# Gated layers in 50 units of 510 tokens across all batches, in place of 56 units of 448

## The chip, the core and the metric

The kernel runs on one core of one Trainium2 chip. The core has five engines with an instruction queue each: PE (matrix multiplication, called TensorE), ACT (ScalarE), DVE (VectorE), POOL (GpSimd) and SP (SyncE), which here issues nearly all DMAs. Sixteen DMA engines carry the transfers. The metric is the device time of one launch in microseconds (us); lower is better. Three runs of the kernel before took 1591.54, 1593.37 and 1595.23 us, median 1593.37.

## The reference

Eight batches of 3136 tokens with 256 columns pass through a filter in the frequency domain and then a gated layer; only the essence is shown.

```python
X = np.fft.rfft(x, axis=1)                      # x: (8, 3136, 256)
y = np.fft.irfft(X * (filt_r + 1j * filt_i), n=3136, axis=1)
h = np.maximum(y @ w_in, 0.0)                   # w_in: (256, 1024)
hp = pad(h, 1 token of zeros at both ends of each batch)
conv_out = sum(conv_w[k] * hp[:, k:k + 3136] for k in range(3))
out = (h / (1 + np.exp(-conv_out))) @ w_out     # w_out: (1024, 256)
```

## The kernel before

The Fourier transforms are done as matrix products in four passes over a batch, each pass in 14 pieces `q`. Pass "1" reads `x` and stores to `a_dram`; pass "2" reads that back, multiplies by the filter (`filt`, three DVE operations and one POOL addition); pass "3" stores to `b_dram`; pass "4" reads that and gives `y`, the input of the gated layer, kept on chip as a coarse and a fine half (`y` is two tiles, and so are the weights `wi`, `wo` and the gated values `g`, so that one product takes three matmuls, `mm3`). An operation of a pass is called by its number below: a 2 is one piece of the second pass.

The first batch is transformed alone (the head). After that the transforms of the following batches are interleaved with the gated layer. The gated layer is cut into units of `SUB` = 448 tokens, seven to a batch and 56 in all, and each unit into eight blocks `f` of 128 hidden columns. One (unit, `f`) is a **step** `m` of the main loop, 448 steps in all. In step `m`

- PE does the transform operations that the table `plan` puts on this step, then the six matmuls of `inner` (128x450, into a PSUM bank of `ps_h`, four of them), then `project` for step `m - 6`: three matmuls for each tile of 128 tokens, accumulated over the eight `f` in the two banks of `ps_o`.
- ACT does `relu` and `centre` for step `m - 1`, `sigmoid` for `m - 2`, `round_g` for `m - 3`; DVE does `tap`, `gate`, `tap`; POOL does `rest_g` for `m - 4`. The tile `t` that they share has four buffers, so `centre` waits until `rest_g` of four steps earlier is done.
- At the head of a step, `evacuate` copies the finished `ps_o` of a unit whose last `f` was projected in the step before (DVE, two copies) and SP stores it; then `from_bank` empties the transform banks that the step before filled (DVE for a 2 or a 4, ACT for a 1 or a 3, which SP then stores). There are two such banks, `ps_t`.

448 is 3.5 tiles of 128, so two units share a middle tile: its first 64 columns come from the even unit, the last 64 from the odd one (`split_parts`, tiles `gm`). Even units project three tiles, odd ones four. Within a batch of 56 steps, the 2s stand on every second step and the 3s on those between.

All engines follow the order in which the code is written (`manual_schedule`). SP issues loads ahead: the inputs of five operations ahead (`want_in`), the tables for 1 and 3 three such operations ahead (`want_table`), the filter for the next 2 (`want_filter`). A load that reads what a pass stored is issued only when all 14 stores of that pass have landed (`ready`). A DMA on SP also waits for the DMA eight places before it to land: they share a completion semaphore, DMAHW0 to DMAHW7 in turn.

Of the kernel before, what the change touches and what calls it, by code (L numbers as in the profile page):

```python
# [124 lines left out]
def tile_fft_filter_gated_ffn(  # L125
# [25 lines left out]
    def lo_pool(dst, src, hi):  # L151
        nc.gpsimd.tensor_tensor(out=dst, in0=src, in1=hi.bitcast(F32), op=ALU.subtract)  # L152
# [276 lines left out]
    outv = out.rearrange("b s d -> (b s) d").rearrange("(j t p) d -> j p t d", p=128, t=NT)  # L429
    hs, ts, gs, mids, pos = {}, {}, {}, {}, {}  # L430
    NU = B * NSUB
    HALF = SUB - 3 * 128

    def at(m):

        return (m // NF, m % NF) if 0 <= m < NF * NU else None

    def inner(u, f):
        ps = ps_h.tile([128, 512], F32, name="ps_h")[:, 0:SUB + 2]
        fs = slice(128 * f, 128 * f + 128)  # L440
        yh, yl = ys[u // NSUB]
        us = slice(u % NSUB * SUB, u % NSUB * SUB + SUB + 2)
# [5 lines left out]
        nc.scalar.activation(hs[u, f], hs[u, f], AF.Relu)  # L448

    def centre(u, f):  # L450
        ts[u, f] = t = wp.tile([128, SUB], F32, name="t", bufs=4)
        nc.scalar.activation(t, hs[u, f][:, 1:SUB + 1], AF.Copy, scale=cw[:, 1, f:f + 1])  # L452

    def tap(u, f, k):
        h, t = hs[u, f], ts[u, f]
        nc.vector.scalar_tensor_tensor(out=t, in0=h[:, k:SUB + k], scalar=cw[:, k, f:f + 1], in1=t, op0=ALU.mult, op1=ALU.add)  # L456

    def sigmoid(u, f):
        nc.scalar.activation(ts[u, f], ts[u, f], AF.Sigmoid)  # L459

    def gate(u, f):
        nc.vector.tensor_mul(ts[u, f], hs.pop((u, f))[:, 1:SUB + 1], ts[u, f])  # L462

    def split_parts(u, f):

        if u % 2:
            return ((gs[u, f], slice(0, 384), slice(HALF, SUB)), (mids[u // 2, f], slice(HALF, 128), slice(0, HALF)))
        return ((gs[u, f], slice(0, 384), slice(0, 384)), (mids[u // 2, f], slice(0, HALF), slice(384, SUB)))

    def round_g(u, f):  # L470
        gs[u, f] = [wp.tile([128, 384], F32R, name=f"g{h}", bufs=4) for h in range(2)]
        if u % 2 == 0:
            mids[u // 2, f] = [wp.tile([128, 128], F32R, name=f"gm{h}", bufs=NF) for h in range(2)]
        for g, o, i in split_parts(u, f):
            hi_act(g[0][:, o], ts[u, f][:, i])

    def rest_g(u, f):
        for g, o, i in split_parts(u, f):
            lo_pool(g[1][:, o], ts[u, f][:, i], g[0][:, o])
        del ts[u, f]  # L480

    def project(u, f):
        g = gs.pop((u, f))
        tiles = [[h[:, 128 * k:128 * k + 128] for h in g] for k in range(3)]
        if u % 2:
            tiles = [[h[:] for h in mids.pop((u // 2, f))]] + tiles
        if f == 0:
            pos[u] = [ps_o.tile([128, 512], F32, name=f"po{k}") for k in range(2)]
        for t, (gh, gl) in enumerate(tiles):
            o = pos[u][t // 2][:, t % 2 * D:t % 2 * D + D]  # L490
            first, last = f == 0 and t % 2 == 0, f == NF - 1
            nc.tensor.matmul(o, lhsT=gh, rhs=wo[0][:, f], start=first, stop=False, skip_group_check=True)  # L492
            nc.tensor.matmul(o, lhsT=gh, rhs=wo[1][:, f], start=False, stop=False, skip_group_check=True)  # L493
            nc.tensor.matmul(o, lhsT=gl, rhs=wo[0][:, f], start=False, stop=last, skip_group_check=True)  # L494

    def evacuate(u, f):
        if f < NF - 1:
            return
        t0, nt = (3, 4) if u % 2 else (0, 3)
        for k in range(2):  # L500
            n = min(2, nt - 2 * k)
            ot = wp.tile([128, 2, D], F32, name="ot", bufs=3)
            o, src = ot[:, 0:n].rearrange("p t d -> p (t d)"), pos[u][k][:, 0:n * D]
            if u == NU - 1 and k:
                nc.scalar.activation(o, src, AF.Copy)
            else:
                nc.vector.tensor_copy(o, src)  # L507
            nc.sync.dma_start(out=outv[u // 2][:, t0 + 2 * k:t0 + 2 * k + n], in_=ot[:, 0:n])

    NW = NF * NSUB  # L510
    plan = {}

    def put(m, kind, b, q):
        plan.setdefault(m, []).append((kind, b, q))

    for t in range(1, B):
        w = NW * (t - 1)
        at2, at4 = (10, [44 + 10 * q // NP for q in range(NP)]) if t == 1 else (4, [37 + 17 * q // NP for q in range(NP)])
        used = set(at4)
        for q in range(NP):  # L520
            used |= {at2 + 2 * q, at2 + 3 + 2 * q}
            put(w + at2 + 2 * q, "2", t, q)
            put(w + at2 + 3 + 2 * q, "3", t, q)
            put(w + at4[q], "4", t, q)
        if t == 1:
            for q in range(AHEAD, NP):
                s = (q - AHEAD) * 7 // (NP - AHEAD)
                used.add(s)
                put(s, "1", 1, q)
        free = [s for s in range(53) if s not in used]  # L530
        free = sorted(free + [s for s in range(at2, 53) if s // NF % 2 == 0 and s not in free][::-1][:NP - len(free)])
        if t + 1 < B:
            for q, s in enumerate(free[:NP]):
                put(w + s, "1", t + 1, q)
    order = [(m, op) for m in sorted(plan) for op in plan[m]]
    inputs = [op for _, op in order if op[0] in "124"]
    tables = [op for _, op in order if op[0] in "13"]
# [70 lines left out]
    with tc.manual_schedule(engines=COMPUTE | {mybir.EngineType.SP}):  # L608
# [4 lines left out]
        for m in range(NF * NU + PLAG + 1):  # L613
# [74 lines left out]
```

## Time and profile before

| what | value |
|---|---|
| median of three runs | 1593.37 us |
| profiled execution, device time | 1592.42 us |
| its span, first to last instruction | 1590.6 us |
| instructions | 28686 |
| granted TensorE clock, mean | 0.99 |
| first `inner` matmul | 120.5 us after the start of the span |

The span begins with the head, in which PE often waits, and goes on with 448 steps that are laid end to end on PE. [...] An operation on PE that stands in two parts in the records (transform matmuls of type f32) shows as twice as many rows.

```profile
PEclk9889999999999999999999999999999999999999
```

This row of the page, forty equal slices of the span, says that from the fourth slice on at least nine tenths of the clock were granted.

### The profile page before, as it was taken

How to read it: one execution, taken by the hardware profiler on the slowest of the kernel's cores; microseconds unless marked ns; L12 is line 12 of the kernel's file. 1: busy time of each engine (PE TensorE's matmuls, PEld its weight loads, DVE VectorE, ACT ScalarE, POOL GpSimd, SP SyncE). 2: the span in 40 equal slices, each digit the busy share in tenths (PEclk: the TensorE clock that was granted, in tenths of full speed). 3: DMA queues.
4: the chain of work that ended last, by engine and by line, in shares of the span. 5: the costliest groups of instructions: out<-in, count | busy, mean ns of one | idle time of the engine just before them, and what ended most of it. 6: DMA issues, size and time to landing. Idle time of an engine off the chain costs nothing.

```text
span 1590.6 us, 28686 instructions
## 1 busy us (share of the span) xinstructions
PE 1539.5 (97%) x9648; PEld 1395.2 (88%) x9648; DVE 1195.3 (75%) x1966; ACT 1197.6 (75%) x2623; POOL 877.1 (55%) x1170
## 2 busy tenths in 40 slices
PE   6879999999999999999999999999999999999999
PEld 5778889988899888998899988998889988899998
DVE  5856887578776887768776778667877788877876
ACT  3368668876788667986688766887668966799897
POOL 2523545745565454755556454664556655576554
PEclk9889999999999999999999999999999999999999
DMA  9807555465545664356544555445554445310001
GB/s 271 257 24 236 181 158 163 145 197 174 151 129 145 184 181 143 113 160 192 167 146 125 177 169 165 139 130 176 160 166 125 132 143 173 102 58 24 24 25 37
DMA packets 159866, 229.28 MB, mean 144 GB/s; under 512 B 15807, under 2 KB 108839, under 8 KB 159719
## 3 DMA queue, kind: packets, MB, share of 16 engines
q1 hardware_dynamic: 158759, 226.53, 47.8%
q8 instruction: 77, 1.26, 0.3%
q10 hardware_dynamic: 960, 0.92, 0.2%
q14 instruction: 70, 0.57, 0.1%
HBM read 156.74 MB, written 70.65 MB: 143 GB/s over the span
## 4 chain that ended last, share of the span: by engine, by line
PE 62%; issue 15%; POOL 10%; DVE 5%; DMA 4%; ACT 3%; SPq 0%; POOLq 0%; ACTq 0%; DVEq 0%
PE po L492 8%; PE po L493 8%; PE po L494 8%; PE ps_h L177 8%; PE ps_h L178 8%; PE ps_h L179 8%; POOL g L152 7%; PE ps_t L233 6%; PE ps_t L257 5%; DVE t L456 2%; POOL gm L152 2%; PE ps_t L237 2%; DMA f<-in_filt 1%; DMA rows<-in_x 1%; ACT t L452 1%
## 5 line engine op out<-in xcount | busy, mean ns | idle before, releaser
L456 DVE SCALAR_TENSOR_TENSOR t<-ps_h,cw,t 128x448 f32<-128x448 f32 x896 | 609.1, 680 | 327.9 <-ACT t L452 323.2
L152 POOL TENSOR_TENSOR g<-t,g 128x384 fp32r<-128x384 f32 x448 | 455.4, 1016 | 186.1 <-ACT g L146 75.5
L452 ACT ACTIVATE t<-ps_h,cw 128x448 f32<-128x448 f32 x448 | 284.9, 636 | 243.8 <-POOL gm L152 210.5
L177 PE MATMUL ps_h<-y,wi 128*128 128x450 f32 x896 | 410.1, 458 | 0.0
L492 PE MATMUL po<-wo,g 128*128 128x256 f32 x1344 | 374.5, 279 | 0.5
L493 PE MATMUL po<-wo,g 128*128 128x256 f32 x1344 | 374.1, 278 | 0.0
L494 PE MATMUL po<-wo,g 128*128 128x256 f32 x1344 | 373.6, 278 | 0.0
L249 POOL TENSOR_TENSOR z<-z,v 120x512 f32<-120x512 f32 x112 | 147.1, 1313 | 356.5 <-DVE v L248 325.3
L178 PE MATMUL ps_h<-y,wi 128*128 128x450 f32 x896 | 328.8, 367 | 0.3 <-DVE y L149 0.3
L179 PE MATMUL ps_h<-y,wi 128*128 128x450 f32 x896 | 328.5, 367 | 0.0
L448 ACT ACTIVATE ps_h<-ps_h 128x450 f32<-128x450 f32 x448 | 243.6, 544 | 65.3 <-PE ps_h L179 63.9
L462 DVE TENSOR_TENSOR t<-ps_h,t 128x448 f32<-128x448 f32 x448 | 275.6, 615 | 0.7 <-ACT t L459 0.6
L492 PEld LDWEIGHTS po<-wo,g 128*128 128x128 f32 x1344 | 253.3, 188 | 7.0 <-DVE ot L507 3.1
L493 PEld LDWEIGHTS po<-wo,g 128*128 128x128 f32 x1344 | 252.4, 188 | 3.7
L459 ACT ACTIVATE t<-t 128x448 f32<-128x448 f32 x448 | 254.4, 568 | 1.1 <-DVE t L456 0.9
L494 PEld LDWEIGHTS po<-wo,g 128*128 128x128 f32 x1344 | 253.2, 188 | 0.0
L146 ACT ACTIVATE g<-t 128x384 fp32r<-128x384 f32 x448 | 229.8, 513 | 0.2 <-DVE t L462 0.2
L152 POOL TENSOR_TENSOR y<-z,y 128x448 fp32r<-128x448 f32 x98 | 138.0, 1411 | 121.5 <-ACT y L146 118.9
L177 PEld LDWEIGHTS ps_h<-y,wi 128*128 128x128 f32 x896 | 169.5, 189 | 37.4 <-issue 22.3
L178 PEld LDWEIGHTS ps_h<-y,wi 128*128 128x128 f32 x896 | 170.2, 190 | 34.8 <-issue 22.5
L179 PEld LDWEIGHTS ps_h<-y,wi 128*128 128x128 f32 x896 | 168.6, 188 | 15.4
L152 POOL TENSOR_TENSOR gm<-t,gm 128x64 fp32r<-128x64 f32 x448 | 145.6, 325 | 0.0
(80 smaller groups left out, 1973.4 us busy)
## 6 DMA issues: line engine op xcount, KB each, us to landing
filt<-in_filt SPq DMA_DIRECT2D x98, 512.0 KB, 5.3
tin<-a_dram SPq DMA_DIRECT2D x98, 224.0 KB, 4.3
b_dram<-st SPq DMA_DIRECT2D x98, 224.0 KB, 2.4
tin<-b_dram SPq DMA_DIRECT2D x98, 224.0 KB, 3.1
out<-ot SPq DMA_DIRECT2D x84, 256.0 KB, 2.2
tin<-in_x SPq DMA_DIRECT2D x94, 224.0 KB, 3.8
a_dram<-st SPq DMA_DIRECT2D x94, 224.0 KB, 2.4
tab<-in_i SPq DMA_DIRECT2D x98, 105.0 KB, 4.7
```

What stands on the lines that cost most here:

```text
L152: nc.gpsimd.tensor_tensor(out=dst, in0=src, in1=hi.bitcast(F32), op=ALU.subtract)
L177: nc.tensor.matmul(ps, lhsT=wh, rhs=rh, start=start, stop=False, **kw)
L178: nc.tensor.matmul(ps, lhsT=wh, rhs=rl, start=False, stop=False, **kw)
L179: nc.tensor.matmul(ps, lhsT=wl, rhs=rh, start=False, stop=stop, **kw)
L448: nc.scalar.activation(hs[u, f], hs[u, f], AF.Relu)
L452: nc.scalar.activation(t, hs[u, f][:, 1:SUB + 1], AF.Copy, scale=cw[:, 1, f:f + 1])
L456: nc.vector.scalar_tensor_tensor(out=t, in0=h[:, k:SUB + k], scalar=cw[:, k, f:f + 1], in1=t, op0=ALU.mult, op1=ALU.add)
L459: nc.scalar.activation(ts[u, f], ts[u, f], AF.Sigmoid)
L462: nc.vector.tensor_mul(ts[u, f], hs.pop((u, f))[:, 1:SUB + 1], ts[u, f])
L492: nc.tensor.matmul(o, lhsT=gh, rhs=wo[0][:, f], start=first, stop=False, skip_group_check=True)
L493: nc.tensor.matmul(o, lhsT=gh, rhs=wo[1][:, f], start=False, stop=False, skip_group_check=True)
L494: nc.tensor.matmul(o, lhsT=gl, rhs=wo[0][:, f], start=False, stop=last, skip_group_check=True)
```

## The change

The gated layer runs over all batches in one row of `8 * 3137 - 1` positions: each batch has its 3136 tokens and then one position of padding, whose result is thrown away. The row is cut into units of 510 positions: 49 full ones and a last one of 105. There are 400 steps. A unit of 510 takes 512 columns of `h`, a whole PSUM bank.

- `inner` works on 512 columns, `relu`, `centre`, `tap`, `sigmoid`, `gate`, `round_g` and `rest_g` on 510 or 512 in one instruction each; `split_parts` and the tiles `gm` are gone.
- `tiles_of` cuts a unit into tiles of 128, 128, 127 and 127 tokens, so every full unit projects four tiles. The 127 wide ones are multiplied from slices of `g` that start at columns 256 and 383.
- `evacuate` copies two tiles at a time and stores them with one DMA: 128 rows of 2 times 1 KB, then 127 rows of 2 times 1 KB. Where the end of a batch falls into a pair of tiles, the tiles are stored apart and around the padding.
- Seven units span two batches. For each, `join_tail` (POOL, two copies) and `join_head` (one copy on ACT, one on POOL) put the end of one batch's `y` and the start of the next into a tile of its own, `yx`.
- The transforms of a batch are planned on 48 steps in place of 56, 56 operations as before; the 2s come in a pattern of gaps 2, 2, 2, 2, 1 (for the first such batch 1 and 2 in turn), and steps with two operations are more frequent.

```diff
-SUB = 448
-NSUB = S // SUB
-CH = 2 * SUB
-NT = CH // 128
+UO = 510
+ROW = S + 1
...
+    def place(u):
+        b, tok = divmod(UO * u, ROW)
+        return b, tok, min(UO, LEN - UO * u)
...
+    def join_tail(u):
+        b, tok, n = place(u)
+        joined[u] = [wp.tile([128, KT, UO + 2], F32R, name=f"yx{h}", bufs=1) for h in range(2)]
+        for t, y in zip(joined[u], ys[b]):
+            nc.gpsimd.tensor_copy(t[:, :, 0:ROW + 1 - tok], y[:, :, tok:ROW + 1])
+
+    def join_head(u):
+        b, tok, n = place(u)
+        c = ROW + 1 - tok
+        src, dst = [y[:, :, 1:n + 3 - c] for y in ys[b + 1]], [t[:, :, c:n + 2] for t in joined[u]]
+        nc.scalar.activation(dst[0], src[0], AF.Copy)
+        nc.gpsimd.tensor_copy(dst[1], src[1])
...
     def round_g(u, f):
-        gs[u, f] = [wp.tile([128, 384], F32R, name=f"g{h}", bufs=4) for h in range(2)]
-        if u % 2 == 0:
-            mids[u // 2, f] = [wp.tile([128, 128], F32R, name=f"gm{h}", bufs=NF) for h in range(2)]
-        for g, o, i in split_parts(u, f):
-            hi_act(g[0][:, o], ts[u, f][:, i])
+        gs[u, f] = [wp.tile([128, UO], F32R, name=f"g{h}", bufs=4)[:, 0:place(u)[2]] for h in range(2)]
+        hi_act(gs[u, f][0], ts[u, f])
...
+    def tiles_of(u):
+        n = place(u)[2]
+        if n <= 128:
+            return [(0, n)]
+        assert n == UO
+        return [(0, 128), (128, 128), (256, 127), (383, 127)]
...
     def evacuate(u, f):
...
+            n = part[0][1]
+            ot = wp.tile([128, 2, D], F32, name="ot", bufs=3)[0:n, 0:len(part)]
+            nc.vector.tensor_copy(ot.rearrange("p t d -> p (t d)"), pos[u][k][0:n, 0:len(part) * D])
+            p = UO * u + part[0][0]
+            b, tok = divmod(p, ROW)
+            if tok + len(part) * n <= S:
+                rows = outf[p - b:p - b + len(part) * n].rearrange("(t p) d -> p t d", p=n)
+                nc.sync.dma_start(out=rows, in_=ot)
+                continue
...
+        else:
+            at2, at4 = [2 + 9 * q // 5 for q in range(NP)], [32 + 12 * q // NP for q in range(NP)]
...
+        tails[w + 29] = heads[w + 45] = next(u for u in range(NU) if joins(u) and place(u)[0] == t - 1)
```

Two places show how the order moves. The first is **SP** where a unit of the third batch has been copied out of `ps_o`; `ot` is the copy, `st` a transform result on its way to memory, `tin`, `tab` and `filt` are loads, and in brackets stands what the instruction waits for. Before:

```order
L508 DMA out_0<-ot_3300 128x2x256 [waits DMAHW3_49,DVE_49]
L508 DMA out_0<-ot_3303 128x2x256 [waits DMAHW4_49,DVE_49]
L223 DMA tin_3308<-a_dram2_59 112x512 [waits DMAHW5_49,DMAHW0_49,PE_49]
L557 DMA tab_3377<-in_s1 112x224 [waits DMAHW6_49]
L229 DMA a_dram3_60<-st_3412 112x2x256 [waits DMAHW7_49,Activation_49]
```

Of the changed kernel, step 6 of the second window of 48:

```order
L527 DMA out_0<-ot_3290 128x2x256 [waits DMAHW3_49,DVE_49]
L527 DMA out_0<-ot_3293 127x2x256 [waits DMAHW4_49,DVE_49]
L227 DMA b_dram2_67<-st_3296 112x512 [waits DMAHW5_49,Activation_49]
L221 DMA tin_3304<-in_x 112x512 [waits DMAHW6_49,PE_49]
L590 DMA tab_3307<-in_s1 112x224 [waits DMAHW7_49]
L590 DMA tab_3312<-in_i1 120x224 [waits DMAHW0_49,PE_49]
L227 DMA b_dram2_67<-st_3348 112x512 [waits DMAHW1_49,Activation_49]
L227 DMA a_dram3_60<-st_3351 112x2x256 [waits DMAHW2_49,Activation_49]
L221 DMA tin_3354<-a_dram2_59 112x512 [waits DMAHW3_49,PE_49]
L595 DMA filt_3357<-in_filt 128x1024 [waits DMAHW4_49,DVE_49]
```

The second store of a unit has 127 rows, and more transfers of the transforms follow it closely; the tenth row takes the semaphore of the 127 row store and so waits for it.

The second place is **PE** at the same step. Before, between the end of a projection (`po1`) and the next `inner` (`ps_h`), there is one operation at the corresponding place:

```order
L494 MATMUL po1_3335<-wo0_85,g1_3358 128x256
L233 MATMUL ps_t_3499<-tin_3257,tab_3377 112x256 [waits DMAHW6_49,DMAHW2_49,Activation_49]
L233 MATMUL ps_t_3499<-tin_3257,tab_3377 112x256
L177 MATMUL ps_h_3504<-y0_2836,wi0_83 128x450 [waits DVE_49]
L178 MATMUL ps_h_3504<-y1_2837,wi0_83 128x450
```

Of the changed kernel:

```order
L510 MATMUL po1_3006<-wo0_85,g1_3146 127x256
L231 MATMUL ps_t_3306<-z_3204,tab_3090 112x256 [waits DMAHW7_49,Activation_49,Pool_49]
L231 MATMUL ps_t_3306<-z_3204,tab_3090 112x256
L231 MATMUL ps_t_3311<-tin_3127,tab_3212 112x256 [waits DMAHW6_49,DMAHW1_49,Activation_49]
L231 MATMUL ps_t_3311<-tin_3127,tab_3212 112x256
L175 MATMUL ps_h_3316<-yx0_2227,wi0_83 128x512 [waits DVE_49]
L176 MATMUL ps_h_3316<-yx1_2228,wi0_83 128x512
```

Two operations now stand on one step, each with its own waits for a bank and for loads, and `inner` reads the joined tile `yx`, 512 columns wide.

More of the change, by code (lines that the diff above doesn't have):

```diff
@@ L209, in y_slices @@
         if sl.start == 0:
-            ys[b] = [yps[b % 2].tile([128, KT, S + 2], F32R, name=f"y{h}") for h in range(2)]
+            ys[b] = [yps[b % 2].tile([128, KT, S + 4], F32R, name=f"y{h}") for h in range(2)]
             for t in ys[b]:
                 nc.gpsimd.memset(t[:, :, 0:1].bitcast(F32), 0.0)
-                nc.gpsimd.memset(t[:, :, S + 1:S + 2].bitcast(F32), 0.0)
+                nc.gpsimd.memset(t[:, :, S + 1:S + 4].bitcast(F32), 0.0)
         return (t[:, :, 1:S + 1].rearrange("p k (a c) -> p k c a", c=N2)[:, :, sl] for t in ys[b])
@@ L482, in project @@
     def project(u, f):
[L483 to L486, printed above, removed]
+        gh, gl = gs.pop((u, f))
         if f == 0:
             pos[u] = [ps_o.tile([128, 512], F32, name=f"po{k}") for k in range(2)]
-        for t, (gh, gl) in enumerate(tiles):
-            o = pos[u][t // 2][:, t % 2 * D:t % 2 * D + D]
+        for t, (c, n) in enumerate(tiles_of(u)):
+            o = pos[u][t // 2][0:n, t % 2 * D:t % 2 * D + D]
@@ L491, in project @@
             first, last = f == 0 and t % 2 == 0, f == NF - 1
-            nc.tensor.matmul(o, lhsT=gh, rhs=wo[0][:, f], start=first, stop=False, skip_group_check=True)
-            nc.tensor.matmul(o, lhsT=gh, rhs=wo[1][:, f], start=False, stop=False, skip_group_check=True)
-            nc.tensor.matmul(o, lhsT=gl, rhs=wo[0][:, f], start=False, stop=last, skip_group_check=True)
+            nc.tensor.matmul(o, lhsT=gh[:, c:c + n], rhs=wo[0][:, f], start=first, stop=False, skip_group_check=True)
@@ L496, in evacuate @@
+            nc.tensor.matmul(o, lhsT=gh[:, c:c + n], rhs=wo[1][:, f], start=False, stop=False, skip_group_check=True)
+            nc.tensor.matmul(o, lhsT=gl[:, c:c + n], rhs=wo[0][:, f], start=False, stop=last, skip_group_check=True)
     def evacuate(u, f):
@@ L498, in evacuate @@
             return
-        t0, nt = (3, 4) if u % 2 else (0, 3)
+        tiles = tiles_of(u)
         for k in range(2):
[L501 to L511, printed above, removed]
+            part = tiles[2 * k:2 * k + 2]
+            if not part:
+                continue
[7 more added lines that the diff above has]
+                nc.sync.dma_start(out=rows, in_=ot)
+                continue
+            for t in range(len(part)):
+                b, tok = divmod(p + t * n, ROW)
+                r, end = p + t * n - b, min(n, S - tok)
+                if end > 0:
+                    nc.sync.dma_start(out=outf[r:r + end], in_=ot[0:end, t])
+                if end + 1 < n:
+                    nc.sync.dma_start(out=outf[r + end:r + n - 1], in_=ot[end + 1:n, t])
+    NW = 6 * NF
+    plan, tails, heads = {}, {}, {}
     def put(m, kind, b, q):
@@ L517, in tile_fft_filter_gated_ffn @@
         w = NW * (t - 1)
-        at2, at4 = (10, [44 + 10 * q // NP for q in range(NP)]) if t == 1 else (4, [37 + 17 * q // NP for q in range(NP)])
-        used = set(at4)
-        for q in range(NP):
[L521 to L531, printed above, removed]
-        if t + 1 < B:
-            for q, s in enumerate(free[:NP]):
+        used = [0] * NW
+        if t == 1:
+            at1 = [q // 2 for q in range(NP - AHEAD)]
+            at2, at4 = [8 + 3 * q // 2 for q in range(NP)], [33 + 11 * q // NP for q in range(NP)]
+            for q, s in enumerate(at1):
+                put(s, "1", 1, AHEAD + q)
+                used[s] += 1
+        else:
+            at2, at4 = [2 + 9 * q // 5 for q in range(NP)], [32 + 12 * q // NP for q in range(NP)]
+        for q in range(NP):
+            for s, kind, cost in ((at2[q], "2", 3), (at2[q] + 3, "3", 1), (at4[q], "4", 1)):
+                put(w + s, kind, t, q)
+                used[s] += cost
+        if t + 1 < B:
+            spots = []
+            for q in range(NP):
+                s = min(range(5 if t == 1 else 0, NW - 2), key=lambda s: (used[s], s))
+                used[s] += 2
+                spots.append(s)
+            for q, s in enumerate(sorted(spots)):
                 put(w + s, "1", t + 1, q)
+        tails[w + 29] = heads[w + 45] = next(u for u in range(NU) if joins(u) and place(u)[0] == t - 1)
+        assert NF * tails[w + 29] >= w + NW
     order = [(m, op) for m in sorted(plan) for op in plan[m]]
@@ L620, in tile_fft_filter_gated_ffn @@
             want_in()
+            if m in tails:
+                join_tail(tails[m])
+            if m in heads:
+                join_head(heads[m])
             for op in new:
```

35 lines of the change are left out of this document (17 added, 18 removed).

## The prediction

> **What bounds the kernel now.** I read the page first, then the timeline of PE, the groups by form, the waits, and last the DMA view.
>
> ```profile
> span 1590.6 us, 28686 instructions
> PE 1539.5 (97%) x9648; PEld 1395.2 (88%) x9648; DVE 1195.3 (75%) x1966; ACT 1197.6 (75%) x2623; POOL 877.1 (55%) x1170
> DMA  9807555465545664356544555445554445310001
> ...
> 800.11 0.28 PE L494 MATMUL po<-wo,g 128*128 128x256 f32 x1
> 800.22 1.03 PE L233 MATMUL ps_t<-z,tab 120*112 120x256 f32 x4
> 800.90 0.56 PE L177 MATMUL ps_h<-y,wi 128*128 128x450 f32 x1
> 801.30 0.37 PE L178 MATMUL ps_h<-y,wi 128*128 128x450 f32 x1
> 801.50 0.37 PE L179 MATMUL ps_h<-y,wi 128*128 128x450 f32 x1
> 802.45 0.28 PE L493 MATMUL po<-wo,g 128*128 128x256 f32 x1
> 802.57 0.28 PE L494 MATMUL po<-wo,g 128*128 128x256 f32 x1
> ```
>
> PE is busy 97%, and its starts give the price of each piece: an inner matmul of 450 columns 0.205 us (801.30 to 801.50), a projection of 256 columns 0.116 (802.45 to 802.57). From the projection at 800.11 to the second inner matmul at 801.30 it is 1.19; less 0.116 and 0.205 that leaves 0.87 for one transform operation. The two kinds have nearly the same price per column, so there is no fixed cost per matmul to save. PE waits little:
>
> ```profile
> PEld ps_t L237 <- PE po L494: 17.4, 26, 0.8
> PEld po L492 <- DVE ot L507: 7.6, 17, 0.5
> ...
> 596.81 0.68 DVE L246 TENSOR_TENSOR z<-ps_t,filt 120x512 f32<-120x512 f32 x1
> 598.98 1.27 POOL L249 TENSOR_TENSOR z<-z,v 120x512 f32<-120x512 f32 x1 [3.34 <-DVE v L248]
> 601.18 0.32 POOL L152 TENSOR_TENSOR gm<-t,gm 128x64 fp32r<-128x64 f32 x1
> 601.53 0.64 ACT L452 ACTIVATE t<-ps_h,cw 128x448 f32<-128x448 f32 x1 [2.34 <-POOL gm L152]
> 602.20 0.68 DVE L456 SCALAR_TENSOR_TENSOR t<-ps_h,cw,t 128x448 f32<-128x448 f32 x1 [1.46 <-ACT t L452]
> 603.93 0.68 DVE L246 TENSOR_TENSOR z<-ps_t,filt 120x512 f32<-120x512 f32 x1
> ```
>
> The first row is PE at a 2, waiting for its bank. The timeline shows why: filter on DVE, its addition on POOL, `rest_g` behind it on POOL, `centre` on ACT for the buffer of `t`, the taps and again the filter form a ring of 603.93 − 596.81 = 7.12 us for two steps. PE needs, with 9 matmuls of projection, 2·(6·0.205 + 9·0.116) + 2·0.87 = 6.29; with 12 it needs 6.98. So PE loses up to 0.8 per pair of steps. All such waits make 17.4 + 7.6 = 25.0 us.
>
> **The change part by part.** *PE work.* Inner columns: before 448·6·450 = 1,209,600, after 392·6·512 + 8·6·108 = 1,209,408: the same. Projections: 4704 before, 4728 after, the 24 more in the drain (below). The full units alone have 5,376 columns less, −2.4 us at 0.205/450. No row has 512 columns of this type: by the price per column of the 256 wide ones a matmul costs 0.232, by that of the 450 wide ones 0.233, so ±2.4 over 2352 of them.
>
> *Waits of the ring.* A pair of steps now has 2·(6·0.233 + 12·0.116) + 1.74 = 7.32 us of PE. The ring grows at most by 62/448 of its three taps and gates and its `centre`, (1.97 + 0.64)·0.138 = 0.36, to 7.48. It loses 0.16 at most where it lost 0.8; the 25.0 go. What comes anew: a 2 whose `filt` stands behind `evacuate` on DVE (steps 6 and 22 of a window), the two 4s of step 38 behind the same copies, and a 1 that must wait for the store of the 3 of its own step on ACT. This arrangement is in the trace once, a 4 behind the two copies:
>
> ```profile
> 271.22 1.02 DVE L507 COPY ot<-po 128x512 f32<-128x512 f32 x2 [0.81 <-PE po L494]
> ```
>
> They begin 0.8 us late and hold DVE 1.0, so such a place costs PE 0.5 to 1.5. About two per window, seven windows: 7 to 21, I take 13. Sum of both −12.
>
> *Joins.* In all 10,474 columns are copied on POOL and 3,862 on ACT. By the rows above (POOL 1.27 for 512, ACT 0.64 for 448) that is 26 and 5.5 us, on engines that are busy 55% and 75%: nothing, and 31 if that cover were gone.
>
> *The stores of 127 rows.* This is the part that decides. How is a transfer dealt out to the 16 engines?
>
> ```profile
> DMA packets 159866, 229.28 MB, mean 144 GB/s; under 512 B 15807, under 2 KB 108839, under 8 KB 159719
> q1 hardware_dynamic: 158759, 226.53, 47.8%
> ...
> filt<-in_filt SPq DMA_DIRECT2D x98, 512.0 KB, 5.3
> tin<-a_dram SPq DMA_DIRECT2D x98, 224.0 KB, 4.3
> out<-ot SPq DMA_DIRECT2D x84, 256.0 KB, 2.2
> tab<-in_i SPq DMA_DIRECT2D x98, 105.0 KB, 4.7
> tab<-in_i SPq DMA_DIRECT2D x7, 210.0 KB, 6.8
> m2g<-in_m SPq DMA_DIRECT2D x4, 12.2 KB
> raw<-in_conv_w SPq DMA_DIRECT2D x1, 24.0 KB, 3.5
> ...
> 400.00:700.00 300.00, 296.88 (x1897) 271.23 (x1896) 223.35 (x371) 237.91 (x517) 175.99 (x234) 1.00 0.50 148
> 1444.00:1570.00 126.00, 126.00 (x858) 120.89 (x857) 100.89 (x169) 113.90 (x263) 67.78 (x106) 1.00 0.07 23
> ```
>
> Data packets under 512 B are few: 128 of 192 B (`conv_w`), 224 of 448 B (the `m2` tables) and 224 of 480 B (`s2`). 15807 − 576 = 15231 are left: completion notes, one from each engine that took part. The DMA view counts 959 transfers; 16 notes each would be 15344, which is 113 too many. The 105 transfers of 120 rows (98 + 7) and the four of 28 rows explain it to the unit if 120 rows go to 15 engines and 28 rows to 14: 105 + 4·2 = 113. So the engines get equal shares of rows, as many engines up to 16 as divide the rows. 127 is divided by none but 1: all 254 packets of 1 KB would go through one engine. The same count would come out if shares were rounded up to whole rows (8 rows on 15 engines, 2 on 14); 127 rows would then use all 16. No transfer before tells the two apart; that is the first rival.
>
> [...]
>
> Price: in the last window, where only `out` is stored, 0.07·16·126 us of engine time moved 23 GB/s·126 us = 2.9 MB, 0.050 us per KB; over the whole run 0.478·16·1590.6/226,530 KB = 0.054. So 254 KB hold the engine 12.7 to 13.6 us, where `out` lands in 2.2 now. The engine is already busy half the time (0.50) and takes a share of every other transfer, in order of issue, so whatever SP issues behind the store lands that much later. It is issued 1.0 us after its step begins and the engine is free at 13.7. A transfer behind it needs its own share (0.7 for 224 KB, 1.6 for `filt`), that of those between, and 2.2 − 0.8 = 1.4 to land. A step of PE lasts 2.79 + 0.87 per operation. For step 6 this reads: the reader, first on step 8, is wanted after two operations on step 6, its bank wait and products, and step 7 with one operation: 1.74 + 0.9 + 2.79 + 0.87 + 2.79 + 0.87 = 9.9 us; its table lands after the store, the shares ahead of it and its own: 13.7 + 0.7 + 0.7 + 0.35 + 1.4 = 16.9. The six unit ends of a window, us from the step's start:
>
> - step 6: table of the 1 on step 8, issued two steps ahead: needed 9.9, there 16.9, late 7.0
> - step 14: filter of the 2 on 16; DVE wants it at 13.0, has it at 18.4; its bank is 5.0 late
> - step 22: table for 26 and filter for 25: 3 late
> - step 30: input of the 4 on 33: 11.8, 16.5, late 4.7
> - step 38: input of the 4 on 41: 12.5, 15.8, late 3.3
> - step 46: the last store of pass 1 lands at 15.8, its reader is issued only then and takes 4.3: 12.9, 20.1, late 7.2
>
> Sum 30.2 for a window; five of the seven have this plan, 151. The first window, with its 2s closer, comes by the same reckoning to 7.8 + 7 + 10 + 1.6 + 7.2 = 34, the last, without 1s, to 1 + 5 + 2.8 + 3.3 = 12. Together 197 us. Lower end half of it, 98, if SP runs further ahead than I count; upper end 197 + 90, if the other work that piles up on the engine (half of 12.7 per store) adds 2.2 for each of 41 stores.
>
> *The clock.* Some 25 of these waits exceed 4 us.
>
> ```profile
> 42.61 1.62 PE L319 MATMUL ps<-tab,z 120*128 120x112 f32 x6 [6.11 <-POOL z L249]
> 40.00:60.00 20.00, 17.39 (x77) 14.30 (x78) 18.65 (x30) 6.07 (x12) 12.94 (x10) 0.83 0.77 240
> ```
>
> In the head, after PE had waited 6.1 us (until 42.6), the window from 40 to 60 has 0.83 of the clock: 0.17·20 = 3.4 us lost. Per wait 0 to 3.4, I take 1.7: 25·1.7 = 43, bounds 0 and 85.
>
> [...]
>
> *The end.*
>
> ```profile
> 1577.08 0.28 PE L492 MATMUL po<-wo,gm 128*128 128x256 f32 x1
> 1586.49 0.28 PE L494 MATMUL po<-wo,g 128*128 128x256 f32 x1
> 1586.80 0.60 ACT L505 ACTIVATE ot<-po 128x512 f32<-128x512 f32 x1 [4.38 <-PE po L494]
> ```
>
> Now it is 13.5 us from the end of the last inner (1577.08) to the end (1590.6): 84 projections without a pause (9.5), a copy (0.6) and 3.2 of store and close. After, the last full unit's projections end 9.5 + 6·0.68 = 13.6 after its last inner (six short inner blocks lie between, taken at 0.113 a matmul), its copy at 14.4, its store of 127 rows at 14.4 + 12.7 + 1.4 = 28.5, the close 29.6: +16. The short unit of 105 is done before.
>
> *Sum*: 1590.6 − 2.4 − 12 + 197 + 43 + 16 = 1832 span. The profiled execution took 1.8 more than its span and the median of the runs is 1.0 above that: **1835**.
>
> **The rivals.**
>
> *Shares rounded up.* The 127 rows go out on 16 engines; nothing is late. The end then is that of the short unit: last inner 1.6 after the projections (13.6 + 1.6), then the chain of its short operations (between 1.8, a quarter of the ring, and all of it, 7.1; taken 3.7), copy and close 3.7: 22.6, +9.1. 1590.6 − 2.4 − 12 + 9.1 = 1585.3, **1588** as a median, between 1576 and 1596 with the bounds above. This is the other side, faster; it decides if `out` of 127 rows lands in 2 to 3 us, and it turns slower only if the new bank waits pass 18 us. For it: no count excludes it. Against: it deals unequal shares, which no transfer of the trace needs.
>
> *One engine, but the loads are ahead of it.* SP issues early enough in most steps; only step 46, where a reader waits for a store, and the end pay: 1590.6 − 14.4 + 6·7.2 + 16 = 1635, **1638**. Against: tables are issued three operations ahead, two steps where steps hold two operations.
>
> *PE pays for 127 columns and odd starts.* 2352 projections have narrower weights.
>
> ```profile
> L494 PEld LDWEIGHTS po<-wo,g 128*128 128x128 f32 x1344 | 253.2, 188 | 0.0
> L237 PEld LDWEIGHTS ps_t<-tin,s_sb 112*120 112x120 f32 x182 | 26.5, 182 | 18.1 <-PE po L494 17.4
> ```
>
> Loads of 120 columns (182 ns) are no longer than those of 128 (188), so nothing; 5 ns each would be 12 us, which would turn the first rival to 1600.
>
> **How the numbers follow.** One engine with late loads 0.78, own range 1690 to 1950 (low: half the lateness and no clock loss, 1590.6 − 14.4 + 98 + 16 = 1690; high: 287 of lateness and 85 of clock would be 1964, and both at their end at once is not likely, so 1950). Shares rounded up 0.14, of which 0.10 is faster by over 0.2%, 0.02 within and 0.02 slower. One engine hidden 0.08. Measurements of this kernel differ by about 0.2%. The range 1625 to 1950 holds nearly all of the first and the third case. Faster 0.10, same 0.02, slower 0.88.
>
> **What would show it.** Stores of `out` with 254 KB landing in over 13 us; waits of PE and DVE for DMA (`tab`, `tin`, `filt`) at unit ends, which hardly exist now; about 46·15 fewer notes of under 512 B than 16 per transfer; PEclk under 0.95 between 120 us and 1400; and no row of 26 waits at the 2s. I am wrong if `out` lands in about 2 us throughout, or if it lands late and PE doesn't wait for loads.

## The result, and the profile after

The changed kernel takes 1833.38 us, median of four runs (1832.85 to 1834.37), against 1594.12 (1591.54 to 1595.23) before, now also of four runs, one more than the three named at the start: a ratio of 1.150, 95% interval 1.148 to 1.152. It is slower; the forecast was 1835.

| | before | after |
|---|---|---|
| median | 1594.12 us | 1833.38 us |
| span of the profiled execution | 1590.6 us | 1832.4 us |
| start of the span to the first `inner` | 120.5 us | 119.7 us |
| from there to the start of the last block of a full unit's last `inner` (the loop) | 1456.0 us | 1682.0 us |
| from there to the end | 14.2 us | 30.7 us |

The page of the changed kernel, the rows that stand against those of before:

```profile
span 1832.4 us, 26781 instructions
PE 1625.3 (89%) x9384; PEld 1402.4 (77%) x9384; DVE 1182.3 (65%) x1810; ACT 1151.3 (63%) x1989; POOL 817.0 (45%) x695
PEclk8899899999999999999999999998999899999999
DMA packets 159016, 229.16 MB, mean 125 GB/s; under 512 B 14970, under 2 KB 108002, under 8 KB 158882
```

PE has 264 instructions fewer and yet is busy 86 us longer, at 89% of the span instead of 97%: two things have happened, PE waits, and it runs slower when it doesn't. Windows laid exactly over the loop part them. The columns are the window, its length, busy time of PE, PEld, DVE, ACT and POOL, the granted clock, the DMA share and GB/s. Before:

```profile
120.50:1576.50 1456.00, 1437.11 (x9062) 1304.66 (x9061) 1111.84 (x1841) 1140.58 (x2518) 825.65 (x1112) 1.00 0.48 142
```

After:

```profile
119.70:1801.70 1682.00, 1513.15 (x8726) 1304.05 (x8725) 1091.90 (x1659) 1086.96 (x1858) 762.30 (x633) 0.95 0.41 123
384.20:391.00 6.80, 5.43 (x15) 4.45 (x16) 0.00 (x0) 1.91 (x4) 0.00 (x0) 0.50 0.90 254
```

PE is idle 1456.0 − 1437.1 = 18.9 us before and 1682.0 − 1513.2 = 168.9 after: +150. Its busy time grows by 76, at a mean clock of 0.95. The second row shows where: a stretch of half clock behind one wait. In the record of the granted clock the loop has 29 such stretches, each of 3.4, 6.8 or (once) 10.2 us and each at 0.50, 170.7 us in all. With the +16.6 at the end and −0.9 at the start, 150 + 76 + 16.6 − 0.9 is the whole difference of 241.8.

What PE waits for, in the view of waits (us in total, times, longest):

```profile
PE ps_t L255 <- DMA tin<-b_dram: 49.9, 13, 8.1
PE ps_t L231 <- DMA tab<-in_s: 40.9, 8, 7.6
PE ps_t L235 <- DMA tin<-a_dram: 33.1, 6, 7.1
PE ps_t L235 <- issue: 22.6, 7, 5.3
DVE z L244 <- DMA filt<-in_filt: 53.9, 12, 11.4
```

None of the first four rows has its like before, where these two rows hold PE's largest sum and its longest wait in the loop:

```profile
PE ps_t L237 <- PE po L494: 13.0, 26, 0.6
PE ps_t L233 <- DVE z L597: 1.2, 2, 0.7
```

The first three rows of after are waits for loads, and nearly all stand two to four steps behind the unit ends. The fourth names no releaser: in each of its seven cases PE starts just as DVE is done with its filter on a bank, and in four of them, 16.8 of the 22.6 us, DVE had waited for `filt` just before (the fifth row). In the longest, DVE waits 8.44 us for `filt`, its third filter operation ends at 433.09 us, and PE starts at 433.20, after 5.34 idle. One of the waits for a load close by, step 6 of the window that the order in the section on the change shows. SP first (an `x2` joins neighbouring rows):

```profile
369.64 1.00 SPq L527 DMA_DIRECT2D out<-ot  x2
370.73 7.92 SPq L227 DMA_DIRECT2D b_dram<-st  x1
378.75 0.37 SPq L221 DMA_DIRECT2D tin<-in_x  x1
379.17 0.68 SPq L590 DMA_DIRECT2D tab<-in_s  x1
379.94 0.45 SPq L590 DMA_DIRECT2D tab<-in_i  x1
```

And PE:

```profile
378.63 1.03 PE L231 MATMUL ps_t<-z,tab 120*112 120x256 f32 x4
385.57 2.02 PE L231 MATMUL ps_t<-tin,tab 112*112 112x256 f32 x4 [5.92 <-DMA tab<-in_s]
```

Behind the store of 127 rows the next issue takes 7.92 us in place of some 0.35. The table that is wanted at 379.7 is issued only at 379.2, and lands late: of the 232 packets of the two tables (896 B each) all but 15 are done by 382.4, and these last run from 384.9 to 385.4, behind the 254 packets of the store (12 in half a microsecond from 373 us on, by which their end is estimated near 384). PE stands 5.9 us, and then needs 2.02 for four matmuls that took 1.03 before the wait. The packets of the trace between 373.5 and 378.5 are 11 to 12 of 1 KB in every half microsecond, one after another, 0.042 us each, at a DMA share of 0.07: about one engine of sixteen at work, the others at rest.

### The profile page after: what moved, and what is told of

It is laid out like the page before. It is cut to its first block, busy times and chain, and to the rows that moved or that the text cites. A ratio compares the mean times of both kernels' runs of the same rounds, so it can differ in the third digit from the quotient of the medians.

```text
span 1832.4 us, 26781 instructions
## 1 busy us (share of the span) xinstructions
PE 1625.3 (89%) x9384; PEld 1402.4 (77%) x9384; DVE 1182.3 (65%) x1810; ACT 1151.3 (63%) x1989; POOL 817.0 (45%) x695
## 2 busy tenths in 40 slices
DMA packets 159016, 229.16 MB, mean 125 GB/s; under 512 B 14970, under 2 KB 108002, under 8 KB 158882
## 4 chain that ended last, share of the span: by engine, by line
PE 60%; DMA 20%; issue 9%; POOL 4%; ACT 4%; DVE 2%; SPq 1%; POOLq 0%; ACTq 0%; DVEq 0%
PE ps_h L175 8%; PE ps_h L176 8%; PE ps_h L177 8%; DMA tin<-b_dram 7%; PE po L508 7%; PE po L509 7%; PE po L510 7%; PE ps_t L231 7%; DMA a_dram<-st 5%; PE ps_t L255 4%; PE ps_t L235 4%; POOL g L150 3%; DMA tab<-in_s 2%; DMA tab<-in_i 1%; DMA tin<-a_dram 1%
## 5 line engine op out<-in xcount | busy, mean ns | idle before, releaser
L478 DVE SCALAR_TENSOR_TENSOR t<-ps_h,cw,t 128x510 f32<-128x510 f32 (+1 forms) x800 | 588.5, 736 | 420.9 <-ACT t L474 418.1
L150 POOL TENSOR_TENSOR g<-t,g 128x510 fp32r<-128x510 f32 (+1 forms) x400 | 503.9, 1268 | 238.3 <-ACT g L144 215.1
L469 ACT ACTIVATE ps_h<-ps_h 128x512 f32<-128x512 f32 (+1 forms) x400 | 233.0, 583 | 364.6 <-PE ps_h L177 364.4
L508 PE MATMUL po<-wo,g 128*128 128x256 f32 (+2 forms) x1576 | 451.7, 287 | 0.7 <-DVE ot L522 0.5
L509 PE MATMUL po<-wo,g 128*128 128x256 f32 (+2 forms) x1576 | 450.1, 286 | 0.0
L510 PE MATMUL po<-wo,g 128*128 128x256 f32 (+2 forms) x1576 | 445.8, 283 | 0.0
L474 ACT ACTIVATE t<-ps_h,cw 128x510 f32<-128x510 f32 (+1 forms) x400 | 272.3, 681 | 130.0 <-POOL g L150 96.1
L175 PE MATMUL ps_h<-y,wi 128*128 128x512 f32 (+1 forms) x688 | 338.5, 492 | 0.0
L508 PEld LDWEIGHTS po<-wo,g 128*128 128x128 f32 (+2 forms) x1576 | 304.1, 193 | 19.9 <-ACT t L474 1.5
L509 PEld LDWEIGHTS po<-wo,g 128*128 128x128 f32 (+2 forms) x1576 | 303.2, 192 | 17.9
L510 PEld LDWEIGHTS po<-wo,g 128*128 128x128 f32 (+2 forms) x1576 | 303.4, 192 | 0.6 <-POOL g L150 0.5
L176 PE MATMUL ps_h<-y,wi 128*128 128x512 f32 (+1 forms) x688 | 278.6, 405 | 0.3 <-DVE y L147 0.3
L177 PE MATMUL ps_h<-y,wi 128*128 128x512 f32 (+1 forms) x688 | 278.7, 405 | 0.0
L484 DVE TENSOR_TENSOR t<-ps_h,t 128x510 f32<-128x510 f32 (+1 forms) x400 | 268.5, 671 | 0.9 <-ACT t L481 0.8
L144 ACT ACTIVATE g<-t 128x510 fp32r<-128x510 f32 (+1 forms) x400 | 245.2, 613 | 4.4 <-PE po L509 4.0
L481 ACT ACTIVATE t<-t 128x510 f32<-128x510 f32 (+1 forms) x400 | 245.4, 613 | 2.1 <-DVE t L478 2.0
```

The source lines that it names most:

```text
L175: nc.tensor.matmul(ps, lhsT=wh, rhs=rh, start=start, stop=False, **kw)
L176: nc.tensor.matmul(ps, lhsT=wh, rhs=rl, start=False, stop=False, **kw)
L177: nc.tensor.matmul(ps, lhsT=wl, rhs=rh, start=False, stop=stop, **kw)
L474: nc.scalar.activation(t, hs[u, f][:, 1:n + 1], AF.Copy, scale=cw[:, 1, f:f + 1])
L478: nc.vector.scalar_tensor_tensor(out=t, in0=h[:, k:place(u)[2] + k], scalar=cw[:, k, f:f + 1], in1=t, op0=ALU.mult, op1=ALU.add)
L484: nc.vector.tensor_mul(ts[u, f], hs.pop((u, f))[:, 1:place(u)[2] + 1], ts[u, f])
```

## The experiments

Each starts from the changed kernel unless it says otherwise. Idle and busy are PE's in the loop, read from a window as above. The ratios are to runs of the kernel before that were taken beside each (medians 1592.57 to 1594.12).

| run | what | median us | ratio to before (95%) | idle | busy | end |
|---|---|---|---|---|---|---|
| after | | 1833.4 | 1.150 (1.148–1.152) | 168.9 | 1513.2 | 30.7 |
| `e1_split16` | 127 rows as 112 + 15 | 1601.1 | 1.006 (1.005–1.007) | 16.8 | 1438.5 | 23.4 |
| `e2_two_engines` | 127 rows as 122 + 5 | 1626.0 | 1.021 (1.019–1.023) | 32.4 | 1446.5 | 25.0 |
| `e3_act_queue` | issued by ACT | 1755.8 | 1.102 (1.100–1.105) | 115.2 | 1487.7 | 30.4 |
| `e4_pool_queue` | issued by POOL | 1693.0 | 1.063 (1.061–1.065) | 71.1 | 1466.2 | 36.6 |
| `e5_before_127` | before, 128 rows as 127 + 1 | 1810.9 | 1.137 (1.135–1.139) | 162.2 | 1500.1 | 25.1 |

### Only the number of rows: `e1_split16`

```diff
-                nc.sync.dma_start(out=rows, in_=ot)
+                cut = 112 if n == 127 else n
+                nc.sync.dma_start(out=rows[0:cut], in_=ot[0:cut])
+                if cut < n:
+                    nc.sync.dma_start(out=rows[cut:n], in_=ot[cut:n])
```

The parts of a store around the end of a batch are cut into a multiple of 16 rows and the rest in the same way.

> The changed kernel with each store of 127 rows cut into 112 and 15 rows (odd remainders at the ends of batches likewise), nothing else. Theory 'one engine' (127 rows go out through one DMA engine, which holds it 10.7 us, and the loads behind it come late): the waits of PE for DMA at the unit ends go, about 150 us of waits and 72 us of clock with them, and the long end shrinks by 10 us or more; 1585 to 1610 us, clock 0.99. Rival 'plan' (two operations on a step and 48 steps per batch make the loads too late by themselves, the store is incidental): most of the waits stay, above 1750 us.

1601.12 us. The same place in its timeline of SP, step 6 of the same window:

```profile
330.04 1.08 SPq L528 DMA_DIRECT2D out<-ot  x2
331.17 0.48 SPq L530 DMA_DIRECT2D out<-ot  x1
331.74 0.33 SPq L227 DMA_DIRECT2D b_dram<-st  x1
332.17 0.40 SPq L221 DMA_DIRECT2D tin<-in_x  x1
332.61 0.42 SPq L595 DMA_DIRECT2D tab<-in_s  x1
```

No issue is held; the table is out 2.6 us after the unit's first store, where it was 9.5. The loop:

```profile
118.70:1574.00 1455.30, 1438.48 (x8726) 1252.12 (x8725) 1090.21 (x1659) 1087.60 (x1858) 764.96 (x633) 1.00 0.48 142
```

Idle and clock are those of before. So 232 of the 239 us that the change costs come only with stores of such row counts, and the plan of 48 steps, the joins and the columns of 512 by themselves cost no more than the 7 that are left. Theory "one engine" holds, "plan" falls.

### The same store in the kernel before: `e5_before_127`

```diff
-            nc.sync.dma_start(out=outv[u // 2][:, t0 + 2 * k:t0 + 2 * k + n], in_=ot[:, 0:n])
+            dst = outv[u // 2][:, t0 + 2 * k:t0 + 2 * k + n]
+            cut = 128 if k else 127
+            nc.sync.dma_start(out=dst[0:cut], in_=ot[0:cut, 0:n])
+            if cut < 128:
+                nc.sync.dma_start(out=dst[cut:128], in_=ot[cut:128, 0:n])
```

> The kernel before with the first store of each of its 56 units cut into 127 rows and 1 row, nothing else: units, plan and order stay. Theory 'one engine': the 127 rows hold one engine 10.7 us 56 times, and loads behind them come late here too, though with more lead as a step has one operation: 1650 to 1790 us, with waits for tab, tin and filt that were not there. Rival 'plan' (only the order of the changed kernel, with two operations on a step, makes a store of 10.7 us hurt): 1593 to 1610 us.

1810.86 us, beyond the upper end of the range that was expected. In the timeline of SP one of the 56 places; the row of 7.45 us is the one row of 2 KB behind the 127:

```profile
405.75 0.25 SPq L510 DMA_DIRECT2D out<-ot  x1
406.05 7.45 SPq L512 DMA_DIRECT2D out<-ot  x1
413.60 0.41 SPq L510 DMA_DIRECT2D out<-ot  x1
414.11 0.40 SPq L229 DMA_DIRECT2D b_dram<-st  x1
```

The store alone is enough, and the older plan, with its one operation a step, protects only a little better: 162.2 us idle, (162.2 − 18.9)/56 = 2.6 us for each such store against (168.9 − 16.8)/46 = 3.3 in the changed kernel. "More lead" was wrong above all for the filter, for which DVE waits in its view of waits

```profile
DVE z L246 <- DMA filt<-in_filt: 127.5, 21, 7.1
```

where it waits 53.9 us in the changed kernel. Both kernels ask for it only one 2 ahead.

### Half the time on the engine: `e2_two_engines`

```diff
-                nc.sync.dma_start(out=rows, in_=ot)
+                cut = 122 if n == 127 else n
+                nc.sync.dma_start(out=rows[0:cut], in_=ot[0:cut])
+                if cut < n:
+                    nc.sync.dma_start(out=rows[cut:n], in_=ot[cut:n])
```

> The changed kernel with each store of 127 rows cut into 122 and 5 rows; 122 is divided by 2 and by no other number up to 16. If the engines up to 16 that divide the rows take part, 244 packets go through two engines and hold each 5.2 us in place of 10.7. Theory 'cover': the loads have a lead of about 5 us before PE misses them, so each wait shrinks by 5.5 us, from 6.0 to 0.5 and the rest to nothing, and no wait is long enough to lower the clock: 1595 to 1625 us. Rival 'load of the engine': what is lost goes with the time that the engines are held, so half of it stays: about 1700 to 1720 us.

```profile
121.80:1600.70 1478.90, 1446.50 (x8725) 1256.93 (x8724) 1090.44 (x1659) 1086.32 (x1858) 764.71 (x633) 0.99 0.47 139
```

1626.02 us, 1 above the range of "cover". With 122 packets on each of two engines in place of 254 on one (122·0.042 = 5.1 us, an estimate by the time of one packet above, in place of 10.7), 10% of the idle time that the store brought is left ((32.4 − 16.8) / (168.9 − 16.8)), and five stretches of low clock of the 29. So the loss is not in proportion to the time that engines are held. That a lead of some 5 us hides the first half fits, but it is not shown alone: the edit also frees SP, which here has five issues of over 2 us, the longest 4.18, where the changed kernel has 36 of over 6. Which of the two gave how much was not separated.

### Another queue: `e3_act_queue` and `e4_pool_queue`

```diff
-                nc.sync.dma_start(out=rows, in_=ot)
+                queue = nc.scalar if n == 127 else nc.sync
+                queue.dma_start(out=rows, in_=ot)
```

> The changed kernel with the stores of 127 rows issued from ACT's queue in place of SP's; they still have 127 rows. Theory 'in order' (the engine works off what is handed to it in order of issue, whatever the queue; what counts is that it is held): 1815 to 1840 us, as before the edit. Rival 'queue' (an engine takes its queues in turn, so a load's share waits only for as much of the store as it is long itself; only loads of the same queue stand behind the store): the waits for loads nearly go, the long end stays: 1600 to 1650 us.

1755.76 us: between the two, so neither was right. The packets show the store slowed beside SP's queue. Near 361 to 366.5 us ACT's queue moves 4 to 7 packets per half microsecond beside those of SP's queue, and 11 to 12 once SP's queue is empty. That fits the rival's "in turn". But SP's queue is empty because SP waits:

```profile
360.36 0.45 SPq L221 DMA_DIRECT2D tin<-a_dram  x1
373.01 0.35 SPq L596 DMA_DIRECT2D filt<-in_filt  x1
```

In the view of SP's waits:

```profile
SPq L227 <- DMA out<-ot: 98.3, 11, 12.6
SPq L591 <- DMA out<-ot: 84.7, 13, 13.6
SPq L596 <- DMA out<-ot: 70.5, 6, 12.4
SPq L221 <- DMA out<-ot: 63.1, 7, 10.5
```

The store leaves ACT at 355.7, SP issues seven more transfers, and the eighth, `filt`, has the store's semaphore and waits until it has landed at 372.6. In this run ACT's store stands in the same turn of eight semaphores as SP's DMAs. So one hold (SP kept in its issue) is exchanged for another (SP kept at a semaphore), and 317 us of SP's time go there in these four rows.

> The changed kernel with the stores of 127 rows issued from POOL's queue in place of SP's, still whole. [...] Theory 'one engine on any queue': the store holds one engine as on ACT's queue, loads there share it in turn, but no DMA of SP uses its semaphore and SP never waits for it: 1630 to 1700 us. Rival: what the software queue costs POOL (455 us of its 1602 are idle in the profile with cut stores) pushes rest_g and the filter's addition back: over 1720 us.

For this run `nc.gpsimd` stands for `nc.scalar` in the same edit; its page lists POOL's queue as `q0 software_dynamic`. 1692.95 us, "one engine on any queue". The DMA view has for the store

```profile
out<-ot POOLq DMA_DIRECT2D x46, 254.0 KB, 19.6
```

a landing after 19.6 us. Its 64 packets of data (63 of 4 KB, one of 2) follow one another without overlap for 15 us, although sixteen completion notes per store are in the trace: here the data went one packet at a time, whatever the notes count. (The expectation has a wrong number: with cut stores POOL is busy 819.7 of 1597.4 us, so 778 are idle.) POOL pays 3.62 us for an issue that the timeline shows at 350, and the end grows to 36.6 us. With SP free of holds and of the semaphore, 71.1 us of idle time are still left. How much of them is the held engine and how much POOL's 46 issues was not separated.

### What is left with the cut stores

With the stores cut the kernel is still 0.6% slower than before. Two places looked to be had, the bank waits at the unit ends and the 9 us more at the end.

```diff
-            nc.vector.tensor_copy(ot.rearrange("p t d -> p (t d)"), pos[u][k][0:n, 0:len(part) * D])
+            src = pos[u][k][0:n, 0:len(part) * D]
+            if k and any(op[0] in "24" for op in old):
+                nc.scalar.activation(ot.rearrange("p t d -> p (t d)"), src, AF.Copy)
+            else:
+                nc.vector.tensor_copy(ot.rearrange("p t d -> p (t d)"), src)
```

> The changed kernel with the cut stores (112 and 15 rows), and at unit ends where a 2 or a 4 was done in the step before, the second copy of ps_o on ACT in place of DVE. Theory 'two copies ahead of the filter' (the waits of PE at steps 22 and 38 of a window are DVE's 1.4 us of copies): about 0.6 us less at each of them, 6 to 8 us in all, 1593 to 1597 us. Rival 'ACT': the copy on ACT delays a store of the same head or centre as much as it helps DVE: 1600 to 1604 us.

1602.24 us (ratio 1.006, 1.005 to 1.007): the rival. The idle time of PE in the loop is 1456.1 − 1436.9 = 19.2 us, 2.4 more than without the copy on ACT; PE now waits 1.2 us each at two steps of a window.

```diff
+    def begin(u):
+        return LEN - UO * (NU - u) if u else 0
...
-        b, tok = divmod(UO * u, ROW)
-        return b, tok, min(UO, LEN - UO * u)
+        b, tok = divmod(begin(u), ROW)
+        return b, tok, UO if u else LEN - UO * (NU - 1)
```

> The changed kernel with the cut stores and the unit of 105 positions first in place of last. Theory 'end' (with cut stores the end is 9 us longer than before because the last chain of short operations follows the last full unit): the end is again about 14 us after the last inner starts, and the short steps at the start are filled by transforms: 1591 to 1595 us. Rival: the short unit costs at the start what it cost at the end, as PE has too little beside its chain there: 1599 to 1603 us.

1607.96 us (1.010, 1.009 to 1.011), beyond the rival's range too. The end is 15.1 us as expected, but the start reads

```profile
121.40:160.00 38.60, 35.96 (x138) 28.32 (x137) 12.86 (x35) 18.93 (x52) 4.42 (x8) 0.69 0.77 229
```

a mean clock of 0.69 where the short steps stand, 0.31·38.6 = 12 us. What brings the clock down there was not tried.

> Both edits, the copy on ACT and the short unit first, on top of the cut stores. If both theories hold the gains add up: 1584 to 1590 us, 0.2 to 0.5% faster than the kernel before. If both rivals hold: 1598 to 1604 us.

1609.49 us (1.011, 1.010 to 1.013): both edits, no gain, and above both ranges. In the loop of its profile the clock was down for 3.4 us only, so the 12 us of the run before are not what a short start must cost. Here PE waits instead: in its trace up to 160 us 4.2 us for tables and 2.8 for a bank that waits for DVE.

```diff
+    SHORT = 46
+
+    def begin(u):
+        return UO * u if u <= SHORT else LEN - UO * (NU - u)
...
-        b, tok = divmod(UO * u, ROW)
-        return b, tok, min(UO, LEN - UO * u)
+        b, tok = divmod(begin(u), ROW)
+        return b, tok, begin(u + 1) - begin(u)
```

> The changed kernel with the cut stores and the unit of 105 positions as unit 46 of 50 (steps 368 to 375, where PE has no transforms), in place of last. Theory 'end': beside full projections of the unit before and full inners of the unit behind, the short steps leave PE without pauses, but for six steps in which DVE's 2.2 us a step set the pace in place of PE's 1.75: 3 to 4 us lost there, 9 gained at the end: 1594 to 1598 us. Rival: a short unit costs its chain wherever it stands, as it did at the start: 1600 to 1608 us.

1601.42 us (1.005, 1.003 to 1.007), no better than at the end. The loop, now with the short unit in it, and the end together are 1465.1 + 15.1 = 1480.2 us; with the short unit last they are 1455.3 + 23.4 = 1478.7. The reason stands in the timeline of PE, here of the changed kernel:

```profile
1817.67 0.27 PE L175 MATMUL ps_h<-y,wi 128*128 128x108 f32 x1
1817.78 0.28 PE L176 MATMUL ps_h<-y,wi 128*128 128x108 f32 x1
1817.89 0.28 PE L177 MATMUL ps_h<-y,wi 128*128 128x108 f32 x1
```

A matmul of 108 columns costs 0.11 us from start to next start, about as much as one of 256 (0.116), and not the 0.049 of its share of 450. The eight short steps are 48·0.11 + 24·0.116 = 8.1 us of work on PE, and work can't be hidden by moving it. What was taken for the latency of a chain was nearly all that. The prediction's "no fixed cost per matmul" was read from 256 and 450 columns (0.116 and 0.205 us); the 0.11 at 108 columns doesn't follow it. Its own sum had the short blocks at 0.113 a matmul and was right in that.

```diff
-                s = min(range(5 if t == 1 else 0, NW - 2), key=lambda s: (used[s], s))
+                s = min(range(5 if t == 1 else 0, NW - 2), key=lambda s: (used[s] + 4 * (t > 1 and s % NF == NF - 2), s))
...
-            at2, at4 = [2 + 9 * q // 5 for q in range(NP)], [32 + 12 * q // NP for q in range(NP)]
+            at2, at4 = [2 + 9 * q // 5 for q in range(NP)], [32 + (12 * q + 2) // NP for q in range(NP)]
```

> The changed kernel with the cut stores, and from the third batch on two numbers of the plan changed: no 1 on a step at whose head a unit is copied out (they go to steps 15, 17 and 19 in place of 6, 22 and 30), and two 4s on steps 33 and 39 in place of 32 and 38. Theory 'unit ends' (the bank waits that are left, 0.7 to 1.0 us at steps 6 and 38 of a window, belong to operations that share a step with the copies): about 1.4 and 0.7 us less per window, five to six windows: 8 to 11 us less than with cut stores alone, 1590 to 1594 us. Rival, as with the copy on ACT: they turn up at another step: 1599 to 1604 us.

1597.17 us (1.003, 1.002 to 1.004), between the two ranges, 4 less than with the cut stores alone and the best of the changed kernels. But the loop reads

```profile
118.30:1569.10 1450.80, 1434.53 (x8726) 1251.25 (x8725) 1089.55 (x1659) 1086.75 (x1858) 764.71 (x633) 1.00 0.48 142
```

with 16.3 us idle, as before the edit (16.8): the waits turned up at another step, 1.7 us once in a window, so the reason given is not what brought the 4 us. They are in PE's busy time (1438.5 to 1434.5). The profile with the cut stores alone has one stretch of 3.4 us at a clock of 0.50 in the loop, behind a wait of 2.05 us, and this one has none: 1.7 us. Why the rest went is open.

> Both edits on top of the cut stores, the plan and the short unit as unit 46. If both theories hold: 1583 to 1589 us, 0.3 to 0.6% faster than the kernel before. If neither holds: 1600 to 1610 us.

1600.26 us (1.005, 1.003 to 1.006): neither. No version beat the kernel before.

## Why the prediction was right, point by point

**The store goes through one engine: shown.** The count of notes answers to the unit. Of the 14970 packets under 512 B of the changed kernel 576 are data as before, 14394 are notes, of 4 B each. Before, the 112 stores of `out` took 16 each, which leaves 15231 − 1792 = 13439 for all else. By "as many engines up to 16 as divide the rows" the changed kernel's stores give 46·1 for those of 127 x 2, 45·16 for those of 128 x 2, 4·16 for single ones of 128, 3·1 of 127, and 122 for the parts around the batch ends and the last 105 rows (102 rows 6, 125 rows 5, 99 rows 11, and so on): 955, and 13439 + 955 = 14394. Shares rounded up would have given 690 more for the 46 stores alone. The run with 122 and 5 rows answers too: 2 + 5 notes in place of 1 for each of the 46 stores are 276 more, and 14970 + 276 = 15246 is what its page counts. The sign "landing in over 13 us" can be read at the end of the program, where the view gives no landing but the packets do: the last store of 127 rows is issued at 1817.3 us and its note stands at 1830.9. So the counts decide between the two readings that the trace of before left open, for the one that the sum was reckoned with.

**The loads are late: right in kind and place, forecast too high by a fifth to nearly a third.** In the window from 565 us on, the six unit ends cost 6.1, 5.0, 2.0, 4.4, 2.8 and 5.1 us of waiting for loads; forecast were 7.0, 5.0, 3, 4.7, 3.3 and 7.2, 25.4 against 30.2. One term was too dear: 254 packets took 0.042 us each where nothing shares the engine, 10.7 us, not the 12.7 that the mean over a whole window gave. That alone is 2 us at each of the six places, 12 in the window and more than the 4.8 that are missing, so something else made the loads later than reckoned; SP's holds (below) would do so, but this was not separated. In the whole loop 168.9 − 16.8 = 152 us of idle time come from the stores, where the sum had 197.

**The clock: the wrong size.** 1.7 us for each of 25 waits, 43 in all, was the term that was mis-sized most. PE's busy time grew by 76 us, and with cut stores it is 1438.5 again, so 75 of them come with the waits, 2.6 for each of the 29 stretches. The clock stood at 0.50 for 6.8 us behind 19 of the waits, for 3.4 behind nine and for 10.2 behind one; and it came behind shorter ones too: 21 waits were over 4 us, and seven of the 29 stretches followed waits of 2.0 to 3.0 us. The prediction's own row had shown 3.4 us lost behind one wait, and no row gave a reason to halve it. The upper bound of 85 was closer than the middle. No run shows the 1.7 of the sum as the price of a wait; in its place the changed kernel shows the 2.6 for a stretch.

**The end: right.** +16.6 us against +16, and by the path that was forecast: the note of the last store of 127 rows stands at 1830.9 us, one of the short unit's store at 1831.2, and the program closes.

**The waits of the ring: half right.** With cut stores PE's 26 waits of 13.0 us at the 2s, listed behind `po` before, are gone, and the rows that have come are these:

```profile
PE ps_t L235 <- issue: 3.9, 3, 1.4
PE ps_t L231 <- ACT st L226: 3.4, 5, 0.7
PE ps_t L255 <- PE ps_t L255: 2.9, 6, 0.5
```

But idle time fell by 2.1 us only (18.9 to 16.8), where −25.0 and +13 gave −12. This step failed in size. Both rows whose sum is 25.0 are of PEld, the weight loads, and not of PE; PE itself was idle for 18.9 in the whole loop, so no more than that could go. And the waits that are left with the cut stores cost 17 rather than 13.

**Why the total hit 1835 so closely.** Idle time grew by 150 us where 197 − 12 = 185 stood in the sum, and −35 of waiting and +32 of clock cancel. Each of the two was inside its bounds; the total's nearness is luck. The rival "shares rounded up", made true by cutting the stores, was put at 1588 and came out at 1601.1: its span is 12.1 us above the forecast, 10 for the ring's waits and 3.8 for PE's busy time (+1.4 instead of −2.4), less 1.8 at the start. So the change without its store would have been slower as well, by 0.6%.

**Where the mechanism was too simple.** "In order of issue" was said of the engine. In fact SP itself is kept. In the changed kernel 36 issues took over 6 us, each directly behind a store of 127 rows of 2 KB, 297 us in all; before, one took over 2 us (2.17). The loads are late because they are not issued (the table of step 6 until 379.2 us), and then because the rest of the store is still ahead of them (the last packets of that table and the one behind it run to 385.4). The outcome is much the same, as both end with the store.

## What to carry to other kernels

Look at the row count of each transfer before its bytes: 127 rows in place of 128 made a store of 254 KB hold one engine 10.7 us, and cutting it into 112 and 15 gave back 232 of 239 us. What hurt here was not the transfer but what its queue issued next, so ask of each slow transfer which loads follow it and how much lead they have: with two engines held some 5 us each (the estimate above) a tenth of the added idle time was left here; with one held 10.7 us it was 152 us of waiting, and 75 more through the clock. Moving the slow transfer to another queue gave back only a part (1755.8 and 1693.0 us against 1833.4), the smaller part where the first queue still waited for its semaphore.

## What the runs showed of the hardware that was not expected

In the changed kernel an issue on SP directly behind 254 packets for one engine took about 8.2 us (7.4 to 8.7 in 36 cases), and in that time some 136 of the 254 were done (390 packets of 1 KB in a typical hold, 256 of them the 128 row store's). So about 118 were still to come when it went through. With 122 packets on each of two engines only five issues of the whole run took over 2 us. What holds the issue was not shown.

The clock fell to 0.50 behind waits as short as 2.0 us, in the changed kernel's loop for 3.4 us (nine times), 6.8 (19 times) or 10.2 (once), and once, with the short unit first, for 23.9 us in which PE was busy nine tenths of the time (35.96 of the 38.6 us of the window above, at a mean clock of 0.69).
